# Gate loads moved to GpSimd's queue, and the state update cut into quarter products

## The chip, the cores and the metric

The kernel runs on one core of one Trainium2 chip. The time is the device time of one execution in microseconds (us); the median of the runs counts. The engines are TensorE (PE, matmuls), VectorE (DVE), ScalarE (ACT), GpSimd (POOL) and SyncE (SP, which here only issues DMAs). Each runs its own instructions in order and waits on semaphores. DMAs issued by any of them run on the core's 16 DMA engines.

## The reference

Two blocks, one after the other. The first is an mLSTM cell over 4 batches, 8 heads, 768 tokens and 40 values per head. The second, a mixture of depths, sends the 128 tokens with the highest score of each batch through a two-layer network and adds the result.

```python
for t in range(S):
    m_new = np.maximum(f_gate[:, :, t] + m, i_gate[:, :, t])
    f_stab = np.exp(f_gate[:, :, t] + m - m_new)
    i_stab = np.exp(i_gate[:, :, t] - m_new)
    C = f_stab * C + i_stab * np.einsum('bhd,bhe->bhde', vt, kt)
    n = f_stab * n + i_stab * kt
    denom = np.maximum(np.abs((n * qt).sum(-1)), 1.0)
    y[:, :, t] = sigmoid(o_gate[:, :, t]) * (C @ qt) / denom
...
scores = x @ w_gate                        # x is y as (batch, token, 320)
for b in range(B):
    top_idx = the 128 highest scores of batch b
    ye = np.maximum(x[b, top_idx] @ w1, 0.0) @ w2
    out[b, top_idx] = x[b, top_idx] + sigmoid(scores[b, top_idx])[:, None] * ye
```

## The kernel before, in words

The recurrence is computed in chunks. There are 12 steps n (4 batches, 3 pieces of 256 tokens); in a step the 256 tokens lie as two column blocks c of 128 partitions, and each block is two halves r of 64 tokens. The gate factors of all tokens are computed once at the start (`gate_rows`, `gate_cols`).

Per step these functions are called, all in a hand-written order:

- `load(n)` (lines 77 to 81) issues the loads of v, k and q on SP, and `load_o(n)` (71 to 75) the two loads of the output gate, each 128 partitions by 8 heads by 40 values of 4 bytes, 160 KB. k and q have four buffers each, and so have v and the gates (`o_t`, NO = 4). The table `queue` (616 to 618) says in which step which loads are issued; SP works it off in order, so that a gate's loads stand between the loads of v, k and q of different steps.
- `weigh(n)` (239 to 245), on GpSimd: v times its gate factors, written into `wv_t`, in two instructions, one for each half r. In `wv_t` the values of half r stand in column block r (41 columns: 40 values and a one); the rest is zero, so that a product over 128 tokens keeps the two halves apart in 82 columns.
- `turn(n, "kT")` and `turn(n, "qT")`: transposes of k and q on TensorE, copied out by ScalarE. `fill` puts idle matmuls in front of some.
- `update(n)` (259 to 269), on TensorE: the products of k and the weighted values. For each block c, pair of heads p and head j of the pair one matmul with 128 tokens, 64 key columns (40 and zeros) and 82 value columns. `states(n)` (271 to 289), on VectorE, adds the four of them to the running state, one after the other.
- `scores`, `masked`, `read`, `attend`, `divide`: scores of keys and queries, the mask, the read of the states (`read`, line 322: 40 rows, 64 columns, 41 columns), the product with the weighted values, and the division.
- `sigmoid(n)` (247 to 250) on ScalarE takes the gates; `output(n)` (349 to 355) on GpSimd multiplies them in, and `store(n)` (357 to 362) on GpSimd issues the two stores of the step, 160 KB each, 64 partitions by two rows of 1280 bytes.
- `router(n)`, `ranks`, `select`, `numbers`: scores, ranks and indices of a batch, once its three steps are done. `fetch(b)` (512 to 517) on GpSimd gathers the chosen rows from the output; `fetched`, `layer1`, `layer2`, `weighed` are the network, and `add(b)` scatters the result.

In step n `update(n + 1)` and `weigh(n + 2)` are issued; in steps 5, 7 and 8 `weigh(n + 2)` comes after the step's output and store (`behind`, line 675). The network of batch 0 runs in step 6, with its gather issued on GpSimd at the end of step 4; that of batch 1 in steps 8 and 9, its gather issued in step 6; that of batch 2 at the end, its gather issued in step 9.

In PSUM the pool `ps_u` has one buffer, a tile called pU of two banks, taken anew for each use: the columns of the gates, the updates, `picked` and some of `layer1`. The warm-up matmuls of the start (line 97) write a tile of the pool `ps_h`.

Of the kernel before, what the change touches and what calls it, by code (L numbers as in the profile page):

```python
# [9 lines left out]
FP = mybir.dt.float32  # L10
# [16 lines left out]
def _fast(ctx, tc, q, k, v, i_gate, f_gate, o_gate, w_gate, w1_in, w2_in, out):  # L27
# [3 lines left out]
    PE, DVE, ACT, POOL, SP = nc.tensor, nc.vector, nc.scalar, nc.gpsimd, nc.sync  # L31
    B, H, S, D = q.shape
    BH, NP, D1, DM, DP = B * H, H // 2, D + 1, H * D, 64
    NS = S // 256
    N = B * NS
    NF = w1_in.shape[1] // 128
    NB, NO = 4, 4
# [8 lines left out]
    ps_u = ctx.enter_context(tc.tile_pool(name="ps_u", bufs=1, space=PSUM))  # L46
    ps_t = ctx.enter_context(tc.tile_pool(name="ps_t", bufs=2, space=PSUM))
    ps_h = ctx.enter_context(tc.tile_pool(name="ps_h", bufs=1, space=PSUM))

    k_t = [const.tile([128, 2, H, DP], FP, name=f"k{n}") for n in range(NB)]  # L50
    q_t = [const.tile([128, H, 2 * D], FP, name=f"q{n}") for n in range(NB)]
    qw_t = [const.tile([128, 2, H, DP], FP, name=f"qw{n}") for n in range(2)]
    wv_t = [const.tile([128, 2, H, 2, D1], FP, name=f"wv{n}") for n in range(3)]
    v_t = [const.tile([128, 2, H, D1], FP, name=f"v{n}") for n in range(NB)]
    o_t = [const.tile([128, 2, H, D], FP, name=f"o{n}") for n in range(NO)]
    so_t = [const.tile([128, 2, H, D], FP, name=f"so{n}") for n in range(3)]
    G = NS * BH
# [13 lines left out]
    def load_o(n):  # L71
        b, s = divmod(n, NS)
        for c in range(2):
            a = s * 256 + c * 128
            SP.dma_start(out=o_t[n % NO][:, c], in_=o_gate[b, :, a:a + 128, :].rearrange("h p d -> p h d"))  # L75

    def load(n):

# [4 lines left out]
    for t, src in ((f_sb, f_gate), (i_sb, i_gate)):  # L83
        for s in range(NS):
            e = SP if t is f_sb and s < NS - 1 else ACT
# [3 lines left out]
    hot = const.tile([128, 128], FP, name="hot")  # L89
# [4 lines left out]
    DVE.memset(m[0:BH], -BIG)  # L94
    flags = gate.tile([128, 1 + B], FP, name="flags")
    DVE.memset(flags, 0.0)
    warm = ps_h.tile([128, 2, 512], FP, name="warm", tag="h")
    for i in range(WARM):
        PE.matmul(warm[:, i % 2, 0:128], hot, hot, start=True, stop=True)
    load_kv(0, k_t, k)  # L100
    load_q(0)
    load_kv(0, v_t, v)
# [92 lines left out]
    def gate_cols():  # L195
        dz = gate.tile([G, 128], FP, name="dz")
        DVE.tensor_scalar(out=dz.rearrange("b (j e) -> b j e", j=2), in0=odd.unsqueeze(2).to_broadcast([G, 2, 64]),
                          scalar1=E[:, 512:513], scalar2=None, op0=OP.mult)
        DVE.tensor_scalar(out=flags[0:G, 0:1], in0=E[:, 0:1], scalar1=LEAST, scalar2=None, op0=OP.is_ge)
        pc = ps_u.tile([128, 2, 512], FP, name="pU")[:, 0, 0:5 * G].rearrange("s (k g) -> s k g", g=G)  # L200
        for j in range(4):
            e = (256, 384, 0, 128)[j]
            PE.transpose(pc[:, j, :], E[:, e:e + 128], ident[0:G, 0:G])
        PE.matmul(pc[:, 4, 0:G // 2], dz, pairs, start=True, stop=True)
        flat = cols_t.rearrange("s k n b -> s k (n b)")
        DVE.tensor_copy(out=flat[:, 0:2, :], in_=pc[:, 0:2, :])
        DVE.tensor_copy(out=flat[:, 2:4, :].rearrange("s k (b j p) -> s (k b) j p", j=2, p=NP),
                        in_=pc[:, 2:4, :].rearrange("s k (b p j) -> s (k b) j p", j=2, p=NP))
        DVE.tensor_copy(out=cols_t[:, 4, :, 0:BH // 2], in_=pc[:, 4, 0:G // 2].rearrange("s (n b) -> s n b", n=NS))

    state = {}
    pending = {}
# [26 lines left out]
    def weigh(n):  # L239
        pending.setdefault(n, {})  # L240
        b, s = divmod(n, NS)
        for r in range(2):
            o = slice(64 * r, 64 * r + 64)
            (DVE if n == 0 and r else POOL).tensor_tensor(out=wv_t[n % 3][o, :, :, r], in0=v_t[n % NB][o], op=OP.mult,  # L244
                               in1=cols[s][o, 0:2, b * H:b * H + H].unsqueeze(3).to_broadcast([64, 2, H, D1]))
# [6 lines left out]
    def spare(n):  # L252

        g = pending.setdefault(n, {})
        if "pUt" not in g:
            g["pUt"] = ps_u.tile([128, 2, 512], FP, name="pU")
        return g["pUt"][:, :, 384:512]

    def update(n):


        spare(n)
        pU = pending[n]["pUt"][:, :, 0:2 * NP * D1].rearrange("e c (p r x) -> e c p r x", r=2, x=D1)
        for c in range(2):
            for p in range(NP):
                for j in range(2):
                    PE.matmul(pU[64 * j:64 * j + 64, c, p], k_t[n % NB][:, c, 2 * p + j, :], wv_t[n % 3][:, c, 2 * p + j],  # L267
                              start=True, stop=True)
        pending[n]["pU"] = pU

    def states(n, i0=0, i1=4):

        for i in range(i0, i1):
            if n % NS == NS - 1 and i == 3:
                return
            C = work.tile([128, NP, D1], FP, name="C", bufs=12)
            src = pending[n]["pU"][:, i // 2, :, i % 2]
            if (n, i) in state:
                DVE.tensor_tensor(out=C, in0=src, in1=state[n, i], op=OP.add)  # L279
                src = C  # L280
            if i < 3:
                if src is not C:
                    DVE.tensor_copy(out=C, in_=src)
                state[n, i + 1] = C
            else:
                b, s = divmod(n + 1, NS)
                DVE.tensor_tensor(out=C, in0=src, op=OP.mult, in1=cols[s][:, 4, b * NP:b * NP + NP].unsqueeze(2)
                                  .to_broadcast([128, NP, D1]))
                state[n + 1, 0] = C
# [188 lines left out]
    def picked(b):  # L478

        x, d = x_t[b % 2], dep[b]  # L480
        sel = d["sel_f"] = mod.tile([128, 2 * NS, 128], FP, name="sel_f", bufs=1)
        for r in (slice(0, 3), slice(3, 6)):
            DVE.tensor_tensor(out=sel[:, r], in0=iota.unsqueeze(1).to_broadcast([128, 3, 128]),
                              in1=d["cnt"][:, r].unsqueeze(2).to_broadcast([128, 3, 128]), op=OP.is_equal)
        d["xeT"] = mod.tile([128, 3, 128], FP, name="xeT")
        for j, pX in enumerate((ps_u.tile([128, 2, 512], FP, name="pU"), ps_h.tile([128, 2, 512], FP, name="pX", tag="h"),
                                ps_t.tile([128, 1, 512], FP, name="pX", tag="t"))):
            w = min(128, XW - 128 * j)
            for r in range(2 * NS):
                PE.matmul(pX[0:w, 0, 0:128], x[:, r, 128 * j:128 * j + w], sel[:, r, :], start=(r == 0), stop=(r == 2 * NS - 1))  # L490
            w = min(128, DM - 128 * j)
            ACT.copy(out=d["xeT"][0:w, j], in_=pX[0:w, 0, 0:128])
        DVE.tensor_copy(out=d["xeT"][64:128, 2], in_=pX[0:64, 0, 0:128])
        d["three"] = mod.tile([128, 128], FP, name="three", bufs=1)
        DVE.tensor_copy(out=d["three"][64:XW - 256], in_=pX[64:XW - 256, 0, 0:128])
# [44 lines left out]
    def layer1(b, f0):  # L540


        d = dep[b]
        if f0 == 0:
            d["hT"] = mod.tile([128, NF, 128], FP, name="hT")
        early, last = b < B - 2, b == B - 1
        if (early and f0 > 0) or (last and f0 > 0):
            ph = ps_s.tile([128, 2, 512], FP, name="ph", tag="s")
        else:
            ph = ps_u.tile([128, 2, 512], FP, name="pU")  # L550
        ph = ph[:, :, 0:256].rearrange("s i (f e) -> s f i e", e=128)
        for f in range(4):
            for j in range(2):
                PE.matmul(ph[:, f // 2, f % 2, :], w1[:, j, (f0 + f) * 128:(f0 + f) * 128 + 128], d["xeT"][:, j, :],  # L554
                          start=(f < 2 and j == 0), stop=False, skip_group_check=True)
        for f in range(4):
            o = slice(64 * (f % 2), 64 * (f % 2) + 64)
            PE.matmul(ph[:, f // 2, f % 2, :], w1c[o, (f0 + f) // 2, :], d["xeT"][o, 2, :], start=False, stop=True,  # L558
                      skip_group_check=True)
        ACT.activation(out=d["hT"][:, f0:f0 + 4, :].rearrange("s (f i) e -> s f i e", i=2), in_=ph, func=AF.Relu)  # L560
# [45 lines left out]
    def weights():  # L606
# [6 lines left out]
        for h in range(2):  # L613
            SP.dma_start(out=w2[:, 4 * h:4 * h + 4], in_=w2_in[512 * h:512 * h + 512].rearrange("(f p) d -> p f d", p=128))

    queue = {0: (load, 3, load_o, 2), 1: (load, 4, load_o, 3, load, 5, load_o, 4), 2: (load, 6, load_o, 5), 3: (weights, None),
             4: (load, 7, load_o, 6), 6: (load, 8, load_o, 7, load, 9, load_o, 8), 7: (load, 10, load_o, 9),
             8: (load, 11, load_o, 10), 9: (load_o, 11)}
    for n in range(N):
        b, s = divmod(n, NS)  # L620
        more = n + 1 < N
# [5 lines left out]
        if n == 0:  # L627
            update(0)
            states(0)
# [45 lines left out]
        behind = n in (5, 7, 8)  # L675
        if n + 2 < N and not behind:
            weigh(n + 2)
        if n == 0:
            update(1)
            states(1)  # L680
# [31 lines left out]
    b = B - 1  # L712
# [5 lines left out]
    layer2(b - 1)  # L718
    weighed(b - 1)
    picked(b)  # L720
    add(b - 1)
    layer1(b, 0)
# [365 lines left out]
```

## Time and profile before

| What | Value |
|---|---|
| median of 3 runs | 167.65 us (167.13 to 168.6) |
| the profiled execution, its own time | 167.96 us |
| its span, first to last instruction | 166.2 us |
| mean granted TensorE clock | 0.968 |
| busy: TensorE, VectorE, ScalarE, GpSimd | 147.9, 93.1, 89.0, 84.3 us |
| `weigh` on GpSimd (line 244), 23 instructions | 30.5 us |
| stores issued on GpSimd (line 361), 22 | 14.0 us |
| update on TensorE (line 267), 384 records | 16.5 us |
| gate loads issued on SP (line 75), 24 | 160 KB each, 4.7 us to landing (median) |

All quoted lines come from one profiled execution. In a timeline line stand the start, the duration, the engine, the line of the code, the operation, the tile written and the tiles read, and in brackets the idle time of the engine ahead of it with what ended it. Consecutive instructions of one kind are merged: x2 is two of them, with their joint duration. "DMA_DIRECT2D" and "DMA_INDIRECT" on POOL are the time in which GpSimd issues a DMA; the data lands later. A float32 matmul leaves two records.

### The profile page before, as it was taken

The numbers are of one execution on the slowest core, as the hardware profiler recorded it, in microseconds if no ns is written. First come the engines' busy times: TensorE is split into PE (matmuls) and PEld (weight loads), VectorE is DVE, ScalarE is ACT, GpSimd is POOL, SyncE is SP. The second block draws the span as 40 slices with busy tenths as digits, with TensorE's granted clock in tenths as the row PEclk, the third lists the DMA queues.
The fourth block names the chain that finished last, engine by engine and source line by source line (L and its number), as shares of the span: only waits on it lengthen the run. The fifth ranks groups of instructions, "written<-read, shape, count | busy, mean of one in ns | idle before, by whom it ended". The sixth has DMA issues, their size and how long they took to land.

```text
span 166.2 us, 6673 instructions
## 1 busy us (share of the span) xinstructions
PE 147.9 (89%) x2864; PEld 128.4 (77%) x2864; DVE 93.1 (56%) x251; ACT 89.0 (54%) x179; POOL 84.3 (51%) x114
## 2 busy tenths in 40 slices
PE   7989799999989795899999699998799999999900
PEld 7879689898968784887889598867689898898600
DVE  6577364667699858307297702768765929511010
ACT  1577296556798454239586515639556759312000
POOL 7146278959375963306087790099237654122020
PEclk9999999999999999599999999999689999999995
DMA  4999899899989988979999999889113330330110
GB/s 85 196 162 193 134 168 209 165 212 206 210 175 193 189 255 223 336 174 171 168 185 169 234 225 198 132 150 237 20 43 84 45 79 4 79 39 11 38 51 2
DMA packets 91880, 24.31 MB, mean 146 GB/s; under 512 B 88097, under 2 KB 90466, under 8 KB 91842
## 3 DMA queue, kind: packets, MB, share of 16 engines
q1 hardware_dynamic: 89920, 18.75, 62.1%
q0 software_dynamic: 1728, 4.92, 11.7%
q8 instruction: 24, 0.39, 1.0%
q10 hardware_dynamic: 194, 0.13, 0.3%
q14 instruction: 14, 0.11, 0.2%
HBM read 19.20 MB, written 4.59 MB: 143 GB/s over the span
## 4 chain that ended last, share of the span: by engine, by line
PE 52%; DMA 16%; SPq 15%; issue 5%; DVE 4%; ACT 4%; POOL 1%; POOLq 0%; DVEq 0%
DMA k<-in_k_dram 11%; SPq L65 9%; PE pt L232 8%; PE py L570 7%; PE pU L554 7%; PE pU L267 6%; PE pH L332 6%; DMA xe<-out_dram,idx 5%; PE pH L322 4%; PE pS L300 3%; SPq L75 3%; PE ph L554 2%; PE pU L558 2%; ACT sgn L415 2%; PE pX L490 2%
## 5 line engine op out<-in xcount | busy, mean ns | idle before, releaser
L244 POOL TENSOR_TENSOR wv<-v,cols 64x656 f32<-64x656 f32 x23 | 30.5, 1326 | 30.1 <-DMA v<-in_v_dram 17.5
L354 POOL TENSOR_TENSOR x<-y,so 128x320 f32<-128x320 f32 x24 | 20.5, 873 | 22.0 <-DVE y L346 16.8
L236 ACT COPY qT<-pt 128x512 f32<-128x512 f32 x24 | 14.0, 637 | 18.8 <-PE pt L232 18.8
L250 ACT ACTIVATE so<-o 64x320 f32<-64x320 f32 x48 | 22.4, 467 | 0.9
L234 ACT COPY kT<-pt 128x512 f32<-128x512 f32 x24 | 13.2, 585 | 10.2 <-PE pt L232 10.0
L570 PE MATMUL py<-w,hT 128*128 128x320 f32 x64 | 18.3, 436 | 0.0
L332 PE MATMUL pH<-wv,P 128*64 128x82 f32 x384 | 17.4, 246 | 0.0
L267 PE MATMUL pU<-wv,k 128*64 128x82 f32 x384 | 16.5, 237 | 0.9 <-issue 0.9
L410 DVE TENSOR_SCALAR_CACHE_REDUCE cmp<-sb,x 128x768 f32<-128x768 f32 (+2 forms) x14 | 12.0, 858 | 9.0 <-ACT sb L404 8.7
L332 PEld LDWEIGHTS pH<-wv,P 128*64 128x64 f32 x384 | 15.4, 144 | 2.1 <-issue 1.5
L267 PEld LDWEIGHTS pU<-wv,k 128*64 128x64 f32 x384 | 14.5, 137 | 2.9 <-issue 2.0
L279 DVE TENSOR_TENSOR C<-pU,C 128x164 f32<-128x164 f32 x40 | 13.1, 327 | 6.3 <-PE pU L267 5.2
L300 PE MATMUL pS<-qT,kT 40*64 40x64 f32 x768 | 14.8, 222 | 1.4 <-issue 1.0
L361 POOL DMA_DIRECT2D out_dram<-x x22 | 14.0, 639 | 3.3 <-POOL x L354 3.3
L232 PE MATMUL pt<-ident,k 128*128 128x128 f32 x96 | 13.9, 278 | 1.9 <-DMA k<-in_k_dram 1.4
L306 DVE TENSOR_TENSOR P<-pS,mask 128x1024 f32<-128x1024 f32 x12 | 14.6, 1217 | 1.3 <-PE pS L300 1.2
L570 PEld LDWEIGHTS py<-w,hT 128*128 128x128 f32 x64 | 11.8, 191 | 4.4
L300 PEld LDWEIGHTS pS<-qT,kT 40*64 40x64 f32 x768 | 12.7, 134 | 3.1 <-issue 1.7
L369 DVE CUSTOM_DVE_ANT_0 scr<-x,wg 128x320 f32<-128x320 f32 x22 | 13.3, 606 | 2.4 <-POOL x L354 0.8
L232 PEld LDWEIGHTS pt<-ident,k 128*128 128x128 f32 x96 | 10.6, 140 | 4.1 <-PE pt L232 1.4
L322 PE MATMUL pH<-C,qT 40*64 40x41 f32 x704 | 13.7, 229 | 0.0
L232 PE MATMUL pt<-ident,qw 128*128 128x128 f32 x96 | 13.5, 285 | 0.0
(141 smaller groups left out, 226.1 us busy)
## 6 DMA issues: line engine op xcount, KB each, us to landing
k<-in_k_dram SPq DMA_DIRECT2D x24, 160.0 KB, 4.8
q<-in_q_dram SPq DMA_DIRECT2D x12, 320.0 KB, 5.5
v<-in_v_dram SPq DMA_DIRECT2D x24, 160.0 KB, 4.7
o<-in_o_gate_dram SPq DMA_DIRECT2D x24, 160.0 KB, 4.7
out_dram<-x POOLq DMA_DIRECT2D x22, 160.0 KB, 4.0
w<-in_moe_w_dram SPq DMA_DIRECT2D x2, 640.0 KB, 7.8
w<-in_moe_w_dram SPq DMA_DIRECT2D x2, 512.0 KB, 5.9
out_dram<-x SPq DMA_DIRECT2D x2, 160.0 KB, 2.6
```

The source lines that it names most:

```text
L65: SP.dma_start(out=t[n % NB][:, c, :, 0:D], in_=src[b, :, a:a + 128, :].rearrange("h p d -> p h d"))
L232: PE.transpose(pt[:, p, :], src[:, c, 2 * p:2 * p + 2, :].rearrange("s j d -> s (j d)"), ident)
L244: (DVE if n == 0 and r else POOL).tensor_tensor(out=wv_t[n % 3][o, :, :, r], in0=v_t[n % NB][o], op=OP.mult, in1=cols[s][o, 0:2, b * H:b * ...
L250: ACT.activation(out=so_t[n % 3][64 * c:64 * c + 64, r], in_=o_t[n % NO][64 * r:64 * r + 64, c], func=AF.Sigmoid)
L267: PE.matmul(pU[64 * j:64 * j + 64, c, p], k_t[n % NB][:, c, 2 * p + j, :], wv_t[n % 3][:, c, 2 * p + j], start=True, stop=True)
L300: PE.matmul(pS[o, j, c, p, :], kT[e, p, t], qT[e, p, t], start=True, stop=True)
L306: DVE.tensor_tensor(out=P.rearrange(flat), in0=pending[n].pop("pS").rearrange(flat), op=OP.mult, in1=mask.unsqueeze(1).to_broadcast([128, ...
L322: PE.matmul(g["pH"][64 * c:64 * c + 64, NP * j + p, r], g["qT"][e, p, t], state[n, 2 * c + r][e, p, :], start=(c, j) not in g["begun"], st ...
L332: PE.matmul(g["pH"][64 * c:64 * c + 64, NP * j + p], g["P"][:, j, c, p, :], wv_t[n % 3][:, c, 2 * p + j], start=(c, j) not in g["begun"], ...
L354: POOL.tensor_tensor(out=x.rearrange(order, j=2, d=D), in0=pending[n]["y"][:, r].rearrange("s (j p) d -> s j p d", j=2), in1=o.rearrange(o ...
L554: PE.matmul(ph[:, f // 2, f % 2, :], w1[:, j, (f0 + f) * 128:(f0 + f) * 128 + 128], d["xeT"][:, j, :], start=(f < 2 and j == 0), stop=Fals ...
L570: PE.matmul(d["py"], d["hT"][:, f, :], w2[:, f, :], start=(f == 0), stop=(f == NF - 1))
```

## The change

Two things. First, the gate loads of steps 2 to 11 are issued by GpSimd; `load_o(n + 2)` stands in step n right behind the place of `weigh(n + 2)`, and goes out of the table of SP's loads. Those of steps 0 and 1 stay on SP.

Second, `update` multiplies the halves r apart: for each c, p, j and r one matmul of 64 tokens, 40 key columns and 41 value columns. The result of half r goes into PSUM bank r, and `states` reads it there, as 164 neighbouring values. The partitions 40 to 63 and 104 to 127 of the result are no longer written by the update, but still read by `states`; so that something finite stands in them, pU becomes one tile for the whole kernel, and the warm-up matmuls, still twelve, write all of it.

```diff
-            SP.dma_start(out=o_t[n % NO][:, c], in_=o_gate[b, :, a:a + 128, :].rearrange("h p d -> p h d"))
+            (SP if n < 2 else POOL).dma_start(out=o_t[n % NO][:, c], in_=o_gate[b, :, a:a + 128, :].rearrange("h p d -> p h d"))
...
-    warm = ps_h.tile([128, 2, 512], FP, name="warm", tag="h")
+    pU_t = ps_u.tile([128, 2, 512], FP, name="pU")
     for i in range(WARM):
-        PE.matmul(warm[:, i % 2, 0:128], hot, hot, start=True, stop=True)
+        a = i // 2 % 4 * 128
+        PE.matmul(pU_t[:, i % 2, a:a + 128], hot, hot, start=True, stop=True)
...
-        pU = pending[n]["pUt"][:, :, 0:2 * NP * D1].rearrange("e c (p r x) -> e c p r x", r=2, x=D1)
+        pU = pending[n]["pUt"][:, :, 0:2 * NP * D1].rearrange("e r (c p x) -> e r c p x", c=2, x=D1)
         for c in range(2):
             for p in range(NP):
                 for j in range(2):
-                    PE.matmul(pU[64 * j:64 * j + 64, c, p], k_t[n % NB][:, c, 2 * p + j, :], wv_t[n % 3][:, c, 2 * p + j],
-                              start=True, stop=True)
+                    for r in range(2):
+                        o = slice(64 * r, 64 * r + 64)
+                        PE.matmul(pU[64 * j:64 * j + D, r, c, p], k_t[n % NB][o, c, 2 * p + j, 0:D],
+                                  wv_t[n % 3][o, c, 2 * p + j, r], start=True, stop=True)
...
-            src = pending[n]["pU"][:, i // 2, :, i % 2]
+            src = pending[n]["pU"][:, i % 2, i // 2]
...
-    queue = {0: (load, 3, load_o, 2), 1: (load, 4, load_o, 3, load, 5, load_o, 4), 2: (load, 6, load_o, 5), 3: (weights, None),
-             4: (load, 7, load_o, 6), 6: (load, 8, load_o, 7, load, 9, load_o, 8), 7: (load, 10, load_o, 9),
-             8: (load, 11, load_o, 10), 9: (load_o, 11)}
+    queue = {0: (load, 3), 1: (load, 4, load, 5), 2: (load, 6), 3: (weights, None), 4: (load, 7), 6: (load, 8, load, 9),
+             7: (load, 10), 8: (load, 11)}
...
         if n + 2 < N and not behind:
             weigh(n + 2)
+        if n + 2 < N:
+            load_o(n + 2)
```

The other places that took a pU tile of their own (`gate_cols`, `spare`, `picked`, `layer1`) use `pU_t`. Since the diff adds lines, line 512 before is 515 after, and so on.

More of the change, by code (lines that the diff above doesn't have):

```diff
@@ L199, in gate_cols @@
         DVE.tensor_scalar(out=flags[0:G, 0:1], in0=E[:, 0:1], scalar1=LEAST, scalar2=None, op0=OP.is_ge)
-        pc = ps_u.tile([128, 2, 512], FP, name="pU")[:, 0, 0:5 * G].rearrange("s (k g) -> s k g", g=G)
+        pc = pU_t[:, 0, 0:5 * G].rearrange("s (k g) -> s k g", g=G)
         for j in range(4):
@@ L255, in spare @@
         if "pUt" not in g:
-            g["pUt"] = ps_u.tile([128, 2, 512], FP, name="pU")
+            g["pUt"] = pU_t
         return g["pUt"][:, :, 384:512]
@@ L485, in picked @@
         d["xeT"] = mod.tile([128, 3, 128], FP, name="xeT")
-        for j, pX in enumerate((ps_u.tile([128, 2, 512], FP, name="pU"), ps_h.tile([128, 2, 512], FP, name="pX", tag="h"),
+        for j, pX in enumerate((pU_t, ps_h.tile([128, 2, 512], FP, name="pX", tag="h"),
                                 ps_t.tile([128, 1, 512], FP, name="pX", tag="t"))):
@@ L549, in layer1 @@
         else:
-            ph = ps_u.tile([128, 2, 512], FP, name="pU")
+            ph = pU_t
         ph = ph[:, :, 0:256].rearrange("s i (f e) -> s f i e", e=128)
```

## The prediction

> **What bounds the kernel now.** I read the page first, then the chain of waits in order of time, then the timeline of GpSimd (POOL), then single lines of the code for durations.
>
> ```profile
> core 0: 166.2 us, clock 0.968
> PE 147.9 (89%) x2864; PEld 128.4 (77%) x2864; DVE 93.1 (56%) x251; ACT 89.0 (54%) x179; POOL 84.3 (51%) x114
> DMA  4999899899989988979999999889113330330110
> q1 hardware_dynamic: 89920, 18.75, 62.1%
> q0 software_dynamic: 1728, 4.92, 11.7%
> ```
>
> TensorE is busy 89% of the span and GpSimd 51%. The row of tenths says that the 16 DMA engines are full from the second slice of 40 to the 28th (to about 116 us). Whole-span shares mislead here, so the chain comes next.
>
> ```profile
> 52.09 5.59 DMA k<-in_k_dram
> ...
> 60.53 5.37 DMA xe<-out_dram,idx
> ...
> 67.01 3.53 PE pU L554 x16
> ...
> 71.19 1.98 PE ph L554 x16
> ```
>
> Up to 60.5 us the chain runs through loads of k; then it runs through the gather of batch 0's chosen rows (xe, issued by GpSimd in step 4, used in step 6), and from 66 us through TensorE. So that gather is the joint between a stage paced by loads and a stage paced by matmuls. What holds the gather?
>
> ```profile
> 56.17 0.16 DVE L474 SCALAR_TENSOR_TENSOR idx<-pU,off 128x1 int32<-128x1 f32 x1
> ```
> ```profile
> 19.54 2.63 POOL L244 TENSOR_TENSOR wv<-v,cols 64x656 f32<-64x656 f32 x2 [4.46 <-DMA v<-in_v_dram]
> 23.19 1.79 POOL L354 TENSOR_TENSOR x<-y,so 128x320 f32<-128x320 f32 x2 [1.01 <-ACT so L250]
> ...
> 37.45 2.64 POOL L244 TENSOR_TENSOR wv<-v,cols 64x656 f32<-64x656 f32 x2 [1.61 <-DMA v<-in_v_dram]
> ...
> 46.45 2.63 POOL L244 TENSOR_TENSOR wv<-v,cols 64x656 f32<-64x656 f32 x2 [3.04 <-DMA v<-in_v_dram]
> ...
> 53.99 2.92 POOL L244 TENSOR_TENSOR wv<-v,cols 64x656 f32<-64x656 f32 x2 [1.60 <-DMA v<-in_v_dram]
> 57.00 1.70 POOL L354 TENSOR_TENSOR x<-y,so 128x320 f32<-128x320 f32 x2
> 58.99 1.24 POOL L361 DMA_DIRECT2D out_dram<-x  x2 [0.30 <-POOL x L354]
> 60.53 1.12 POOL L515 DMA_INDIRECT xe<-out_dram,idx  x1 [0.30 <-DVE C L279]
> ```
> ```profile
> 63.05 1.16 PE L300 MATMUL pS<-qT,kT 40*64 40x64 f32 x64
> 66.03 0.52 PE L525 MATMUL pX<-ident,xe 128*128 128x128 f32 x3 [1.83 <-DMA xe<-out_dram,idx]
> ```
>
> The index is there at 56.33 (56.17 + 0.16); the "DVE C" beside the gather is only the last semaphore event. The gather starts at 60.53 because GpSimd works in order: weigh(6) from 53.99 (held until v came), output(4), store(4), gather. TensorE has finished the scores of step 6 at 64.2 and stands 1.83 us for the gather. Between 23.19 and 60.53, 37.34 us, GpSimd waited for v only 1.61 + 3.04 + 1.60 = 6.25 us; the other 31.09 us are its own work with the gaps that belong to it. This engine looks half idle, and in this stage it has 17% to spare.
>
> **The change part by part.** *Quarter products.* A step's update was 16 matmuls of 128 rows, 64 key columns and 82 value columns; it becomes 32 of 64 rows, 40 and 41. A float32 matmul has two records.
>
> ```profile
> 32.83 1.35 PE L267 MATMUL pU<-wv,k 128*64 128x82 f32 x32
> 34.11 1.14 PE L322 MATMUL pH<-C,qT 40*64 40x41 f32 x64
> 35.19 1.09 PE L232 MATMUL pt<-ident,qw 128*128 128x128 f32 x8
> ```
>
> Start to start, the old update holds TensorE 34.11 − 32.83 = 1.28 us. The nearest row is the state read: also 41 columns in four quarters of the array, 64 records in 35.19 − 34.11 = 1.08 us. I take 1.08, so 0.20 less per update. The ends: 0.64 if halving the columns halved the time, 2.56 if 64 records went at the old 40 ns each with the two row halves one after the other. Updates before the joint save nothing there, since GpSimd holds it; update(10) lies beside the ranking of batch 2 that the step waits for anyway. Updates 7, 8, 9 and 11 are on the path: 4 × 0.20 = 0.8 us less. The ends give −2.6 and +5.1. The four sums per step on VectorE read 164 values a row as before; the 12 warm-up matmuls only write elsewhere; the one shared PSUM tile moves a few waits but none to an instruction that comes late. These I cost at nothing.
>
> *Gates.* Twenty issues leave SP; two stand on GpSimd behind weigh(n+2) in steps 0 to 4 and 9, and in steps 5, 7 and 8, where weigh comes late, before output(n); in step 6 between weigh(8) and the gather of batch 1. GpSimd is in order, so everything behind them waits: output, store, the next weigh, the gathers. The bytes stay. What does one such issue hold GpSimd for? No row shows 1024 rows of 160 B issued there. The near ones:
>
> ```profile
> L361 POOL DMA_DIRECT2D out_dram<-x x22: 599/632/816, 25.3 to 132.6; - x22
> ```
> ```profile
> L515 POOL DMA_INDIRECT xe<-out_dram,idx x4: 1094/1106/1120, 60.5 to 151.8; - x4
> L583 POOL DMA_INDIRECT out_dram<-yg,idx x4: 1045/1697/1847, 91.2 to 158.7; - x4
> ```
> ```profile
> L86 SPq DMA_DIRECT2D f_sb<-in_f_gate_dram x2: 407/407/407, 0.8 to 1.3; - x2
> ```
> ```profile
> L65 SPq DMA_DIRECT2D k<-in_k_dram x24: 426/926/2916, 1.7 to 106.8; - x24
> ```
>
> A store of 128 rows (64 partitions, two runs of 1280 B) holds GpSimd 0.63 us. If nothing of it goes with the rows, a gate issue costs 0.63; if all of it does, 8 × 0.63 = 5.1 us. On SP, 32 rows took 0.407 and 1024 rows 0.426 at the least, so there rows cost next to nothing, but another generator makes them. On GpSimd the indirect issues, also of 128 rows, run from 1.05 to 1.85, so something beyond a fixed price is there. I take t = 1.5 us: four fifths of 0.63 fixed, one fifth growing eightfold (0.63 × (0.8 + 1.6) = 1.5). It is an estimate, nearest to the same instruction's own row.
>
> [...]
>
> *The sum.* Ten issues stand before the gather of batch 0: pairs for steps 2 to 6. The first pair starts at 22.17 (19.54 + 2.63), where GpSimd otherwise waits to 23.19. With no waits left, the gather starts at 22.17 + 31.09 + 10t = 53.26 + 10t; with v for step 6 no earlier than now, at 60.53 + 2t or later. At t = 1.5 the first is 68.3: 7.7 us late, and from there TensorE is the pace again. The SP issues removed give nothing back on this side, because v is no longer what GpSimd waits for. Next:
>
> ```profile
> 91.19 1.70 POOL L583 DMA_INDIRECT out_dram<-yg,idx  x1 [0.30 <-issue]
> 93.52 1.69 POOL L354 TENSOR_TENSOR x<-y,so 128x320 f32<-128x320 f32 x2 [0.63 <-DVE y L346]
> 95.50 1.30 POOL L361 DMA_DIRECT2D out_dram<-x  x2 [0.30 <-POOL x L354]
> 96.80 2.69 POOL L244 TENSOR_TENSOR wv<-v,cols 64x656 f32<-64x656 f32 x2
> ```
> ```profile
> 101.16 1.35 PE L267 MATMUL pU<-wv,k 128*64 128x82 f32 x32
> ```
>
> In step 7 the pair goes into the 0.63 us before 93.52; weigh(9) would end at 99.49 + 2t − 0.63, and update(9) wants it at 101.16, some 0.4 us earlier by the shorter updates 7 and 8. That costs 2t − 1.9, at t = 1.5 about 1.1 us. The pairs of steps 5 and 8 lie in waits of GpSimd for y; those of 6 and 9 delay gathers that TensorE uses only two steps on. Sum: 7.7 + 1.1 − 0.8 = 8.0 us on the profiled execution's 167.96 (span 166.2): 176.0. That execution lies 0.3 above the median 167.65, so I forecast 175.7 for the median.
>
> **The rivals.**
>
> *Issues stay at the store's price (t = 0.63 to 0.85), and the loads gain.* The late gather is then 60.53 + 1.3 if v comes as now: 167.96 + 1.3 − 0.8 = 168.5, no change. But queue q1 spends 62.1% of 166.2 us on 89,920 packets, 1.18 us of all engines for 1024, while the 30 transfers of q0 (22 stores, 8 indirect) took 11.7%, 0.65 us each. If gate rows go at q0's price, up to 0.53 us is saved ten times before the joint, v comes earlier, and the gather falls to GpSimd's floor, 53.26 + 6.3 = 59.6: 0.9 earlier. If it also lands sooner than the 5.37 us it took, TensorE's whole wait of 1.83 can go. That makes 167.96 − 0.9 − 0.8 = 166.3 down to 165.3, with the offset of 0.3 some 165 to 166. For it speak SP's rows, against it q0's large rows (1280 B where the gates have 160 B). 0.30 for the case: 0.20 ends over 1% faster, 0.10 within.
>
> [...]
>
> *Rows set the price (t over 2.1, up to 5.1).* Then GpSimd is the bound all through the loads: t = 3 gives 22.7 + 4.1 − 0.8, 194; t = 5.1 gives 43.7 + 8.3 − 0.8, 219. It decides from t = 0.9, where 10t passes the present waits. Chance 0.25.
>
> *The quarters do not run beside each other:* +5.1 with cheap issues, 173. The state read, built the same way, speaks against it: 0.05.
>
> That the change isn't what it says can be left out: the built order has the ten pairs on GpSimd, and 32 quarter products a step.
>
> **How the numbers follow.** My forecast, t between 0.85 and 2.1, has 0.40 and its own range 169 to 183 (at 0.85: 1.7 − 0.8; at 2.1: 13.7 + 2.3 − 0.8). Likeliest 175.7. The range goes down to 164.8, to hold most of the faster case, and up to t = 2.75 (20.2 + 3.6 − 0.8), 191; outside lies most of the upper half of the row-priced case, about 0.15, and a little below. One per cent, 1.7 us, is about what a measurement can tell from no change. Faster: 0.20. Within: 0.10 and the lowest 0.03 of my case, 0.13. Slower: 0.37 + 0.25 + 0.05 = 0.67.
>
> **What would show it.** The gate issue on GpSimd in the profile after: 1.5 us (0.6 for the first rival, over 2 for the second). The gather of batch 0 starts near 68, with GpSimd busy without waits for v before it, and TensorE standing longer ahead of the transposes of the gathered rows. Updates of 64 records take about 1.08 us from start to start. I am wrong if the gates' issues are as short as the stores', or if GpSimd still waits for v in steps 2 to 4.

## The result, and the profile after

The changed kernel takes 176.45 us (median of 4 runs, 175.49 to 178.17) beside 167.39 us for the kernel before (4 runs, 166.07 to 168.6): 1.055 times as long, 95% interval 1.044 to 1.066. The execution profiled took 175.49 us, with a span of 173.8 us. The forecast of 175.7 us is close; the way to it was mostly another. Executions more than 1.5% above the fastest of their kernel are left out of the ratios, and the profiles of five experiments (the quarters alone, the gates alone, no gate loads, the late quarters, the cut idle products) are of such executions, so that their waits may be somewhat long.

From the page after: the span, the engines' busy times, the slices of the DMA engines, three DMA queues and the chain.

```profile
span 173.8 us, 7431 instructions
...
PE 144.7 (83%) x3248; PEld 125.9 (72%) x3248; DVE 96.1 (55%) x251; ACT 88.7 (51%) x179; POOL 103.3 (59%) x134
...
DMA  4999999998999999989999994303040630330110
...
q1 hardware_dynamic: 69120, 15.47, 52.9%
q0 software_dynamic: 3008, 8.20, 19.9%
q8 instruction: 27, 0.44, 1.1%
...
PE 75%; issue 12%; ACT 4%; DVE 3%; DMA 2%; POOL 1%; POOLq 0%; DVEq 0%
```

TensorE is busy for 3.2 us less than before and GpSimd for 19.0 us more, and yet neither GpSimd nor a data transfer carries the chain: DMA has 2% of it. What has grown is "issue", time in which an engine waited for nothing that the profile shows. TensorE's waits after (the instruction that waited, what for; us in all, times, the longest) say where:

```profile
PE pH L325 <- issue: 6.3, 3, 2.8
PE pS L303 <- issue: 5.9, 4, 2.8
PE pH L335 <- issue: 2.1, 2, 1.2
...
PE pU L270 <- issue: 1.3, 2, 0.9
```

That is 15.6 us of "issue" on TensorE. Before, the same view gave 1.9 us:

```profile
PE pS L300 <- issue: 1.0, 2, 0.8
PE pU L267 <- issue: 0.9, 1, 0.9
```

Its timeline after, around steps 5 and 6:

```profile
53.30 0.83 PE L270 MATMUL pU<-wv,k 64*40 64x41 f32 x64
53.96 0.44 PE L325 MATMUL pH<-C,qT 40*64 40x41 f32 x16
56.68 0.99 PE L325 MATMUL pH<-C,qT 40*64 40x41 f32 x48 [2.27 <-issue]
...
65.71 0.43 PE L325 MATMUL pH<-C,qT 40*64 40x41 f32 x16
68.93 0.91 PE L325 MATMUL pH<-C,qT 40*64 40x41 f32 x48 [2.79 <-issue]
...
72.09 0.81 PE L303 MATMUL pS<-qT,kT 40*64 40x64 f32 x40
75.29 0.58 PE L303 MATMUL pS<-qT,kT 40*64 40x64 f32 x24 [2.39 <-issue]
75.80 0.55 PE L528 MATMUL pX<-ident,xe 128*128 128x128 f32 x3
```

Two things to see. An update of 64 records takes 53.96 − 53.30 = 0.66 us from start to start, half of the old 1.28. And the stalls fall into the middle of groups of like matmuls, after 16 of 64 or 40 of 64, and the profile shows nothing that they wait for. The transposes of the gathered rows (L528) follow at once: the gather isn't what TensorE stands for.

How many matmul records has TensorE done when it stalls? Counted through the timeline from the first one on, for the stalls of 0.25 us and more (three kernels of the experiments beside it):

```
after                             220 347 474 601 855           1236 1490 1618 1869 1995 2122
quarters alone                    220 347 474 601 855 982 1109  1236 1490 1618 1869 1995 2122 2375
before with small products        601 729 854 982               1618 1745 2502
gates alone                       219 980 1361 1612 1737 1865
before                            219 1865
```

Neighbouring stalls lie 125 to 128 records apart, others at a multiple of that, and they lie at the same counts in kernels that do different work there: at record 1618 the change is in the scores of step 6 (the last stall of the timeline above), the kernel with small products in the read of the states of step 5. So the place isn't set by what is computed, but by how many records have gone by. The queue q8, called "instruction", grows with that count. Before, its line was:

```profile
q8 instruction: 24, 0.39, 1.0%
```

The change adds 3248 − 2864 = 384 records, and three packets to this queue: one for 128 records, of 0.44 MB / 27 = 16 KB (why some stalls lie 125 or 127 apart, no run shows). This points to TensorE running out of its own instructions: the next block hasn't come when the last is used up. The times of q8's packets in the trace fit. The stall at 220 ends 1.31 us after the first packet has landed (15.90 us), the one at 347 1.71 us after the second (19.97), and so on: the nth packet belongs to a count of about 220 + 127 (n − 1), up to 2122 and the sixteenth, and all eleven stalls end 1.3 to 1.7 us after theirs. Before, those at 219 and 1865 end 1.45 and 1.74 us after the first and the fourteenth. The experiments below test it further.

The bill is complete by the scores of step 6, which start at 72.09 us after and 63.05 us before. Two stretches, after and before (the length, the busy time of each engine with its instructions, the granted clock, the DMA share, GB/s):

```profile
0.00:72.09 72.09, 59.27 (x1579) 53.59 (x1579) 42.72 (x113) 39.18 (x71) 51.56 (x81) 0.93 1.12 206
```
```profile
0.00:63.05 63.05, 58.70 (x1355) 52.27 (x1355) 41.87 (x113) 39.24 (x71) 40.26 (x69) 1.00 0.98 183
```

Of the 9.0 us, TensorE's idle time is 8.5 (12.82 less 4.35), its busy time 0.6. The busy time should have fallen by 4.3 us, 7 updates at 0.62 us; the granted clock of 0.93 in place of 1.00 takes that back. The quarter products alone (first experiment) come to the same point at 67.73 us, with the clock still at 1.00:

```profile
0.00:67.73 67.73, 55.50 (x1578) 49.97 (x1578) 45.08 (x113) 38.94 (x71) 40.77 (x69) 1.00 0.97 183
```

There the idle time is 7.9 us more than before (12.23 less 4.35), the busy time 3.2 less, and the delay 4.7 us. So of the 9.0 us of the whole change, 3.8 are the same records taking longer at the lower clock (59.27 beside 55.50; 55.50 / 0.93 would be 59.7). Behind that point the change gains 1.4 us (101.71 us left, 103.15 before); the quarters alone lose 3.3 more (106.47 left).

GpSimd after, the issues of the gates and then its timeline:

```profile
L75 POOL DMA_DIRECT2D o<-in_o_gate_dram x20: 897/926/1585, 21.8 to 125.7; - x20
```
```profile
52.52 1.72 POOL L357 TENSOR_TENSOR x<-y,so 128x320 f32<-128x320 f32 x2 [2.37 <-DVE y L349]
...
59.24 1.83 POOL L75 DMA_DIRECT2D o<-in_o_gate_dram  x2
63.21 1.69 POOL L357 TENSOR_TENSOR x<-y,so 128x320 f32<-128x320 f32 x2 [2.14 <-DVE off L473]
...
66.76 1.11 POOL L518 DMA_INDIRECT xe<-out_dram,idx  x1 [0.30 <-DVE C L282]
```

An issue takes 0.93 us. The gather starts at 66.76, 6.2 us later than before, but GpSimd itself stands 2.37 us and 2.14 us ahead of the last two outputs, for y. (The view names "DVE off" at the second; y is written by the same engine just ahead of it, from a product that TensorE ends at 61.45.) TensorE has become late, and GpSimd with it.

### The profile page after: what moved, and what is told of

Same layout as the page of the kernel before. It is cut to its first block, busy times and chain, and to the rows that moved or that the text cites. A ratio compares the mean times of both kernels' runs of the same rounds, so it can differ in the third digit from the quotient of the medians.

```text
span 173.8 us, 7431 instructions
## 1 busy us (share of the span) xinstructions
PE 144.7 (83%) x3248; PEld 125.9 (72%) x3248; DVE 96.1 (55%) x251; ACT 88.7 (51%) x179; POOL 103.3 (59%) x134
## 4 chain that ended last, share of the span: by engine, by line
PE 75%; issue 12%; ACT 4%; DVE 3%; DMA 2%; POOL 1%; POOLq 0%; DVEq 0%
PE pt L233 13%; PE pH L335 10%; PE pS L303 9%; PE pH L325 7%; PE py L573 7%; PE pU L557 6%; PE pU L270 5%; PE pU L100 3%; PE pt L222 3%; PE ph L557 2%; PE pB L403 2%; PE pU L561 2%; DMA xe<-out_dram,idx 2%; ACT sgn L418 2%; PE pX L493 2%
## 5 line engine op out<-in xcount | busy, mean ns | idle before, releaser
L245 POOL TENSOR_TENSOR wv<-v,cols 64x656 f32<-64x656 f32 x23 | 31.5, 1370 | 11.1 <-DVE cols L207 5.9
L303 PE MATMUL pS<-qT,kT 40*64 40x64 f32 x768 | 15.9, 229 | 6.4 <-issue 5.9
L325 PE MATMUL pH<-C,qT 40*64 40x41 f32 x704 | 15.1, 231 | 6.9 <-issue 6.3
L335 PE MATMUL pH<-wv,P 128*64 128x82 f32 x384 | 17.9, 246 | 2.1 <-issue 2.1
L303 PEld LDWEIGHTS pS<-qT,kT 40*64 40x64 f32 x768 | 13.6, 140 | 8.2 <-issue 6.7
L75 POOL DMA_DIRECT2D o<-in_o_gate_dram x20 | 19.2, 995 | 0.0
L325 PEld LDWEIGHTS pH<-C,qT 40*64 40x64 f32 x704 | 13.5, 138 | 7.8 <-issue 6.9
L372 DVE CUSTOM_DVE_ANT_0 scr<-x,wg 128x320 f32<-128x320 f32 x22 | 14.6, 666 | 1.6
L233 PE MATMUL pt<-ident,qw 128*128 128x128 f32 x96 | 14.9, 303 | 0.0
L418 ACT ACTIVATE sgn<-sb,x 128x768 f32<-128x768 f32 (+2 forms) x16 | 12.8, 801 | 0.4
```

Of the source, the lines that this page charges most:

```text
L75: (SP if n < 2 else POOL).dma_start(out=o_t[n % NO][:, c], in_=o_gate[b, :, a:a + 128, :].rearrange("h p d -> p h d"))
L233: PE.transpose(pt[:, p, :], src[:, c, 2 * p:2 * p + 2, :].rearrange("s j d -> s (j d)"), ident)
L303: PE.matmul(pS[o, j, c, p, :], kT[e, p, t], qT[e, p, t], start=True, stop=True)
L325: PE.matmul(g["pH"][64 * c:64 * c + 64, NP * j + p, r], g["qT"][e, p, t], state[n, 2 * c + r][e, p, :], start=(c, j) not in g["begun"], st ...
L335: PE.matmul(g["pH"][64 * c:64 * c + 64, NP * j + p], g["P"][:, j, c, p, :], wv_t[n % 3][:, c, 2 * p + j], start=(c, j) not in g["begun"], ...
L372: DVE.tensor_tensor_reduce(out=scr, in0=x[:, r, 0:DM], in1=wg, scale=1.0, scalar=0.0, op0=OP.mult, op1=OP.add, accum_out=x[:, r, DM:DM + 1])
```

## The experiments

**1. The two parts alone, and the issues on another engine.** The quarter products with all gate loads left on SP:

```diff
-            (SP if n < 2 else POOL).dma_start(out=o_t[n % NO][:, c], ...
+            SP.dma_start(out=o_t[n % NO][:, c], ...
...
-    queue = {0: (load, 3), 1: (load, 4, load, 5), ...
+    queue = {0: (load, 3, load_o, 2), 1: (load, 4, load_o, 3, load, 5, load_o, 4), ...
...
-        if n + 2 < N:
-            load_o(n + 2)
```

> The quarter products alone; every gate load on SP as before. Theory A (GpSimd's in-order queue is what made the change late): the gather of batch 0 starts near 60.5 us as before, and the time is that of before less four shorter updates, 165 to 167. Theory B1 (TensorE stands for its own instructions, and the gate loads on the GpSimd queue make those come late): the same, 165 to 167, with TensorE's idle time put down to issue at about 2 us as before. Theory B2 (TensorE stands for its instructions because the quarter products have 768 more records to bring in): issue idle near 15 us, time near 175.

174.73 us beside 168.21: 1.030 (1.012 to 1.048). TensorE's waits:

```profile
PE pS L303 <- issue: 7.5, 5, 2.7
PE pH L325 <- issue: 4.4, 3, 1.5
PE pU L270 <- issue: 2.5, 3, 1.4
```

16.6 us of "issue" in all, as in the whole change, without a gate on GpSimd: the stalls come with the quarters, as theory B2 said. (Its 768 are instructions: 384 matmul records more and as many weight loads.)

The gates alone, `update` as before (the table `queue` loses its gate loads, as in the change):

```diff
-            SP.dma_start(out=o_t[n % NO][:, c], ...
+            (SP if n < 2 else POOL).dma_start(out=o_t[n % NO][:, c], ...
...
+        if n + 2 < N:
+            load_o(n + 2)
```

> The gate loads on GpSimd alone; the update as before. Theory A, with the issue at its measured 0.93 us: the gather of batch 0 starts at about 62.4 us, and the time is 168.5 to 170. Theory B1: TensorE's issue idle is near 15 us as in the change, time 174 to 178. Theory B2: issue idle near 2 us, time 168.5 to 170 as in A.

172.69 us: 1.0215 (1.006 to 1.037). GpSimd's timeline, then TensorE's:

```profile
63.28 1.13 POOL L515 DMA_INDIRECT xe<-out_dram,idx  x1 [0.30 <-DVE C L279]
```
```profile
67.50 1.05 PE L300 MATMUL pS<-qT,kT 40*64 40x64 f32 x57 [2.23 <-issue]
70.06 0.87 PE L525 MATMUL pX<-ident,xe 128*128 128x128 f32 x3 [1.52 <-DMA xe<-out_dram,idx]
```

Here the prediction's joint is the real one: the gather starts at 63.28, where its formula gives 53.26 + 10 × 0.93 = 62.6, and TensorE waits for the rows. But TensorE has 6.2 us of "issue" too, with no record more than before, and the time is above the 168.5 to 170 of theories A and B2, while B1's 15 us of "issue" isn't there either. By the ratios the parts cost 5.1 and 3.6 us, 8.7 of the whole's 9.2 (0.055 × 168).

The change with ScalarE in place of GpSimd (`(SP if n < 2 else ACT)`):

> The change, with the gates of steps 2 to 11 issued by ScalarE at the same places. Theory A: GpSimd is as free as before, the gather starts near 60.5 us or sooner, 165 to 168 (ScalarE gets some 20 us of issuing, of which a part may show). Theory B1, if it is the GpSimd queue's way of sending that holds the instructions up: issue idle near 2 us, 165 to 168. Theory B2: issue idle near 15 us, time 174 to 177.

181.61 us: 1.085 (1.075 to 1.095), the worst. An issue took 0.376 us there, at most 1.548, and TensorE waited 4.6 us for a copy of ScalarE (L407, the ranking). "Issue" is 9.7 us, at a granted clock of 0.904; no theory had that, nor the time.

**2. As many records at a slower pace.** The kernel before with each product of `update` cut into two of 41 columns, all 128 rows:

```diff
-                    PE.matmul(pU[64 * j:64 * j + 64, c, p], k_t[n % NB][:, c, 2 * p + j, :], wv_t[n % 3][:, c, 2 * p + j],
-                              start=True, stop=True)
+                    for r in range(2):
+                        PE.matmul(pU[64 * j:64 * j + 64, c, p, r], k_t[n % NB][:, c, 2 * p + j, :],
+                                  wv_t[n % 3][:, c, 2 * p + j, r], start=True, stop=True)
```

> The kernel before, with each update matmul of 82 value columns cut into two of 41 columns and still 128 rows and 64 key columns: as many records as the quarter products have, gates on SP. Theories A and B1: only the update's own time changes, 1.28 us to between 1.3 and 2.6, so 0 to +5 us on the path, issue idle near 2 us. Theory B2: issue idle rises to 10 us or more, time above 174.

174.53 us: 1.0435 (1.034 to 1.053).

```profile
25.22 2.09 PE L268 MATMUL pU<-wv,k 128*64 128x41 f32 x64
27.24 1.14 PE L323 MATMUL pH<-C,qT 40*64 40x41 f32 x64
```

64 records, 27 instruction packets, as in the change, but 2.02 us for an update, and 2.0 us of "issue", as theories A and B1 said; the time rose by 7.3 us (0.0435 × 168), more than their 5. Where TensorE stands less, it works longer: 155.5 us busy, beside 147.9 before and 144.7 in the change. So the number of records and packets alone doesn't make the stalls: 3248 and 27 of them go with 2.0 us of "issue" here and with 15.6 in the change.

**3. No gate loads; another place; only late updates.** The change without the gate loads of steps 2 to 11 (the sigmoids read the gates of steps 0 and 1 again); the gates alone, with `load_o(n + 2)` at the end of the step; the quarters for updates 9 to 11 only, all gates on SP (the diffs show the main lines of each):

```diff
-        if n + 2 < N:
-            load_o(n + 2)
```

> The change with the gate loads of steps 2 to 11 left out (the sigmoids read the gates of steps 0 and 1 instead), so the quarter products stay and the DMA engines have 20 transfers of 160 KB less. Theory B3 (TensorE's instructions come in blocks of 128 records, and the loads on the DMA engines set how soon a block comes): issue idle falls from about 16 us to under 8, time 160 to 167. Theory B2 (the number of records alone): issue idle stays at 12 to 16 us, time 171 to 176. Theory A is silent on the idle time and gives 163 to 166.

```diff
         if n in (6, 9):
             add(n // 3 - 2)
+        if n + 2 < N:
+            load_o(n + 2)
```

> The gate loads alone on GpSimd, at the end of each step behind its store and the gather instead of behind the weighted values; the update as before. Theory A (GpSimd's order ahead of the gather of batch 0 costs the gates' 2 to 5 us): the gather starts near 60.5 to 61.5 us, time 166.5 to 169. If instead the sending through GpSimd's DMA queue costs it (blocks of instructions or loads of k late): 170 to 172 as with the gates alone.

```diff
+    QUARTERS = (9, 10, 11)
...
+        if n not in QUARTERS:
...
+            return
```

> Quarter products for updates 9 to 11 only, where the loads are nearly over; updates 0 to 8 and the gate loads as before. Theory B3: no new issue idle; updates 9 and 11 are some 0.6 us shorter each, so 0.6 to 1.2 us faster than before. Theory B2: some issue idle after 101 us, no gain or up to 2 us slower.

Without the gates: 174.25 us, 1.038 (1.011 to 1.065), with 14.2 us of "issue". This missed what I expected: the DMA engines stay full until some 87 us even so (20 of the page's 40 slices; with the gates on SP, 26 slices, 113 us). Behind the store: 174.14 us beside 168.53, 1.033 by the medians, without an interval; TensorE has 2.4 us of "issue", but now waits 1.6 us for weighted values of GpSimd, and the gather, expected at 60.5 to 61.5, starts at 63.66. So another place on GpSimd's queue only moves the wait; 20 issues at 0.93 us are 18.6 us of its time. Late quarters: 1.007 (0.998 to 1.016), no difference where 0.6 to 1.2 us less was expected, with 0.8 us of "issue". In the profiled executions the stretch from update(9) to the end is shorter, 63.4 us (103.73 to 167.1) beside 65.0 (101.16 to 166.2), near 3 × 0.62, though its clock differs too (0.97 and 0.94). The loss lies ahead of it, where the update is the old one: TensorE stands 4.0 us for the rows of batch 0 in place of 1.8. This version has the one shared PSUM tile as well, which therefore costs nothing that the interval shows.

**4. A test that failed by its design.** The kernel before, each idle product of `turn` cut into four of 32 columns:

```diff
...
-            PE.matmul(t, hot, hot, start=True, stop=True)
+            for a in range(0, 128, 128 // cut):
+                PE.matmul(t[:, a:a + 128 // cut], hot, hot[:, a:a + 128 // cut], start=True, stop=True)
```

> The kernel before, with each of the 16 idle matmuls of steps 1 to 5 cut into four of 32 columns, so that TensorE has the same columns to work through in those steps but 96 records more (19 a step on some 215). Theory B3, with a block of 128 records coming every 4 to 5 us under the loads: up to 0.7 us more a step in steps 1 to 5, 1 to 4 us slower, issue idle up by 1 to 3 us. Other theories: no change, 166 to 169.

178.33 us, 1.072 (1.049 to 1.095), but 1.7 us of "issue" only. A record of 32 columns takes 0.11 us, 16 of them 1.81 us from start to next start; one of 128 columns took 0.12 (12 in 1.45 us, in step 2 of the kernel before).

```profile
22.72 1.97 PE L222 MATMUL pt<-hot 128*128 128x32 f32 x16
24.53 1.29 PE L233 MATMUL pt<-ident,k 128*128 128x128 f32 x8
```

So it added TensorE's own time, and the granted clock fell: the page's row of tenths has a 7 from 22.9 to 27.5 us and a 5 from 36.6 to 45.8. It says nothing on the stalls. It was put right with small products (64 rows, 40 and 41 columns):

```diff
-                fill(pt[:, 0, :], count)
+                for i in range(12 * count):
+                    o = slice(64 * (i % 2), 64 * (i % 2) + 64)
+                    PE.matmul(pt[o, 0, 0:41][0:40], hot[o, 0:40], hot[o, 0:41], start=True, stop=True)
```

> The kernel before, with each of the 16 idle products of 0.26 us ahead of the key transposes of steps 1 to 5 replaced by 12 small ones (64 rows, 40 x 41), 192 records where there were 16, in about the same time of TensorE; the result does not use them. Theory A (late blocks): 176 records more in the loaded stage are 1.4 blocks of 128, at 4 to 5 us each some 6 us of supply against little slack: 'issue' idle rises from 2.2 to 5 to 9 us, and the time by 3 to 7 us. Rival B (it is the quarter products themselves): 'issue' idle stays at 2 to 3 and the time within 2 us.

The expectation counts products; a float32 product leaves two records, so that there are 352 more, 2.75 times 128 (27 packets again). 175.86 us beside 169.02: 1.046 (1.033 to 1.059).

```profile
30.42 2.55 PE L232 MATMUL pt<-hot 64*40 64x41 f32 x121
34.57 0.61 PE L232 MATMUL pt<-hot 64*40 64x41 f32 x21 [1.60 <-issue]
...
70.63 0.80 PE L302 MATMUL pS<-qT,kT 40*64 40x64 f32 x39
73.67 0.60 PE L302 MATMUL pS<-qT,kT 40*64 40x64 f32 x13 [2.23 <-issue]
```

"Issue" rises from 1.9 to 7.1 us, with no quarter of an update anywhere in the kernel, and at the counts listed above. It isn't a clean price: the small products also hold TensorE some 4.5 us longer than the idle ones (from start to next start, about 8.7 us in place of 4.2). The stalls are the test, not the time.

**5. Fewer records.** The quarters alone, without the products that read the states in steps 1 to 5:

```diff
-                        if (n, 2 * c + r) in state:
+                        if (n, 2 * c + r) in state and not 0 < n < 6:
```

> The quarter products alone, gates on SP, with the 152 products that read the states in steps 1 to 5 left out. Their own time is about 20 ns each, 3 us. Theory A: 152 records are 1.2 blocks, 5 to 6 us of supply, so 'issue' idle falls from 16.6 to about 10 and the time by 4 to 7 us from 174.7. Rival B: the stalls stay at 14 to 17 us and the time falls by at most 3 us.

506.82 us, which can't be used: with this data the kernel's own test of its result (its flags) calls a general, slow path behind the fast one. Of the fast part, the first 165 us, TensorE's waits:

```profile
PE pH L325 <- issue: 4.0, 2, 2.6
PE pX L528 <- DMA xe<-out_dram,idx: 3.6, 1, 3.6
PE pS L303 <- issue: 1.4, 2, 1.2
PE pU L270 <- issue: 1.3, 2, 0.9
```

6.7 us of "issue" where the quarters alone had 16.6 with these reads, for 304 records fewer (152 products, two records each). The last scatter starts at 163.0 us instead of 166.8, 3.8 us earlier: short of the 4 to 7 expected, with 3.6 us of waiting for the gather in place of stalls.

**6. Few loads.** The quarters alone, and as a control the kernel before, both without the loads of k, q and v of steps 4 to 11 and of the gates of steps 2 to 11:

```diff
...
+    queue = {0: (load, 3), 3: (weights, None)}
...
+                ACT.activation(out=so_t[...], in_=o_t[n % 2][64 * r:64 * r + 64, c], func=AF.Sigmoid)
```

> The quarter products alone, gates on SP, with the loads of k, q and v of steps 4 to 11 and of the gates of steps 2 to 11 left out (the buffers of earlier steps are read again), so that the DMA engines should be idle from about 45 us but for the weights. Theory A, TensorE's own instructions arrive late, in blocks of 128 matmul records, because they come over the same DMA engines as the data: stalls put down to 'issue' stay until about 40 us and are gone behind that; their sum falls from 16.6 us to 4 to 8, and the time lies at most 3 us above the control that has the same loads left out of the kernel before. Rival A2, a block has a fixed price of 4 to 5 us whatever else moves: the stalls in steps 3 to 6 stay and the sum is over 12. Rival B, the stalls belong to the quarter products and not to any supply: one stall in or behind every update, the sum over 12, in no step with 128 records.

> The control: the kernel before with the same loads left out. All theories: idle time put down to 'issue' at most 2.2 us as in the kernel before; the time falls by what the waits for loaded data cost it, by 5 to 20 us.

167.2 us with quarters, 0.989 (0.977 to 1.002) of the kernel before; 164.9 us without, 0.984 (0.975 to 0.993). The control fell by 4.1 us by the medians, less than the 5 to 20 expected; its "issue" is 1.7 us. Two lines of the page with quarters, its waits, then two of its stretches:

```profile
DMA  4999899995030303130013330030125300330110
...
q8 instruction: 27, 0.44, 1.2%
```
```profile
PE pH L325 <- issue: 2.4, 2, 1.5
...
PE pS L303 <- issue: 1.8, 2, 1.2
...
PE pU L270 <- issue: 1.4, 2, 0.8
```
```profile
32.00:46.00 14.00, 11.78 (x404) 10.62 (x404) 9.54 (x19) 6.64 (x13) 10.56 (x15) 1.00 0.58 191
46.00:60.00 14.00, 12.38 (x406) 11.25 (x399) 11.65 (x31) 11.16 (x22) 9.58 (x10) 1.00 0.22 52
```

The same 27 packets, but 5.9 us of "issue" in place of 16.6, 4.7 of them before 46 us, while the data moves or little later (the DMA row is full to slice 9 and half full in slice 10, some 42 us). From there to 125 us there is no stall of 0.25 us, though from 46 to 60 us 406 records pass in 14 us, 34 ns each. The price of the quarters beside their control is 0.006 in ratio, within the intervals, where it was 0.030 with all loads; by the medians (167.2 and 164.9) it is 1.4%, so that the stalls are the evidence here and not the time. So the same count of records has no fixed price: from 46 to 60 us the quarters alone have stalls of 0.57 and 1.49 us at a DMA share of 0.98, and this kernel has none at 0.22. Between the stalls of the quarters alone at 41.14 and 55.37 us 381 records passed, in 14.23 us: 4.7 us for 127.

## Why the prediction came out as it did

- **The price of an issue, 1.5 us: too high.** 0.93 us (the store beside it still 0.64). Eight times the rows made it 1.45 times as long, 0.29 us more. That a fifth of the store's price grows with the rows was my estimate, which no run shows. SP's issues and GpSimd's go by different queues: with twenty gate loads moved, q1 (hardware_dynamic) has 20,800 packets fewer and q0 (software_dynamic) 1,280 more.
- **The joint, the gather of batch 0, +7.7 us: the step that failed for the sum.** With 0.93 us its own formula gives 62.6 us for the gather, 2.0 late. The gates alone show that (63.28). In the whole change the gather is 6.2 us late because GpSimd waits for TensorE: 2.37 and 2.14 us for y, which the formula, with no waits left, doesn't have (62.6 + 4.5 = 67.1). And TensorE doesn't stand for its rows at all, against what the prediction said would show it. That GpSimd would no longer wait for v was right, from the first pair of issues on.
- **The quarter products, −0.8 us: the sign was wrong.** The update itself is shorter than forecast (0.66, not 1.08 us). But the step costed 32 records more for each update at their time on TensorE alone, and took updates ahead of the joint for free. While the loads run, records took 37 ns each with the stalls between them (14.23 us / 381, the quarters alone), and an update now works off 64 in 0.66 us, 10 ns each. Alone, the quarters cost 5.1 us (2.1 to 8.1 by the interval). Stalls of "issue" aren't among the terms costed at nothing, nor among the rivals. The rival that had the quarters at +5.1 had the size by chance: its mechanism, quarters one behind the other, is refuted by the 0.66 us.
- **Step 7, +1.1 us, and the gain of the loads:** neither shows. Behind step 6 the change gains, and the DMA engines are as full as before (share 1.12 against 0.98 up to step 6), though ten pairs of loads left SP. The first rival, a faster kernel, falls with that.
- **The total** of 8.0 us was right to a per cent by luck: a term too large (7.7 for the gather) stood in for ones that weren't there (the stalls of "issue", 15.6 us beside 1.9, and, in the profiled execution, the lower clock, 0.93 beside 1.00 up to step 6).

Shown by runs: the stalls follow the count of records (the same places in kernels with different work; more with small products, 7.1 us beside 1.9; fewer without the reads, 6.7 beside 16.6), their pace (2.0 us with the halves) and the load on the DMA engines (5.9 us with few loads, beside 16.6). Not shown: what makes a packet come late; those of the change took 0.88 to 1.61 us each. Nor why the gates alone raise "issue" from 1.9 to 6.2 us. Its counts lie 125 to 128 records apart, or at a multiple of that, like the others; but the same issues behind the store gave 2.4 us, so one execution of each doesn't settle it. Not shown either: why the clock falls. In the change it falls behind stalls (0.76 from 40 to 60 us, 1.00 before), but with the cut idle products it fell to 7 tenths in the slice from 22.9 us, with no "issue" stall above 0.43 us ahead of it. No version with all its loads beats the kernel before.

## What to carry to other kernels

Count instructions, not only their time: before cutting a matmul into smaller ones, compare the records per microsecond of that stage with what passes between stalls while data is loading (here 127 records in 4.7 us). "Issue" idle in the middle of a group of like matmuls, at a fixed count of records, was the wait for a packet of queue q8 here. Splitting shortened no whole time in these runs, neither late, where the loads are nearly over, nor with few loads. And when a forecast comes out right, look at whether its joint is where the idle time is.

## What the runs showed of the hardware that was not expected

- TensorE stalls of up to 2.79 us lie at fixed counts of matmul records, some 127 apart; in the change all of 0.25 us and more end by 102 us, while the DMA engines are full (to slice 24 of 40, 104 us). With few loads the same 3248 records pass with 5.9 us of "issue", where the quarters alone have 16.6.
- A matmul record of 32 columns with 128 x 128 weights takes 0.11 us, hardly less than one of 128 columns, 0.12; one of a quarter of the array about 10 ns (64 in 0.66 us; 1.11 us from 45.21 us on, at a granted clock of 0.50).
- On GpSimd a DMA issue of 1024 rows of 160 B takes 0.93 us, one of 128 rows 0.64 us; ScalarE took 0.376 us for the former.
